# First tokens of each batch written by one DMA each from two queues, between the whole rows, and a third pair of half rows inside layer two

## The chip, the core and the metric

The kernel runs on one core of a Trainium2 chip. The core has a matrix engine (PE), a vector engine (DVE), a scalar engine (ACT), GpSimd (POOL) and a sync engine (SP) that here does nothing but issue DMAs; 16 DMA engines move the data. The metric is the device time of one execution in microseconds (us); a kernel's number is the median of its runs. The profile covers one further execution, whose own time stands beside its span.

## What is computed

Causal attention with a cumulative bias over 8 batches, 8 heads, 576 positions and 64 channels, followed by a soft mixture of 8 experts with 4 slots each:

```python
scores = scale * q @ k^T                          # B=8, H=8, S=576, D=64
bias = -(cum[:, None] - cum[None, :])             # cum = cumsum(max(s, 0))
attn = softmax(where(causal, -1e9, scores + minimum(bias, 0)))
x = (attn @ v) reshaped to (4608, 512)            # 4608 = B*S, 512 = H*D
logits = x @ phi                                  # 4608 x 32 slots
slot_input = softmax(logits, axis=0).T @ x        # 32 x 512
slot_out[e] = relu(slot_input[e] @ w1[e]) @ w2[e] # 512 -> 1024 -> 512, 8 experts
return softmax(logits, axis=1) @ slot_out         # 4608 x 512, float32
```

The output is 4608 x 512 x 4 bytes = 9.44 MB. Everything after `slot_out` is a product with 32 rows for each token, and the writing of the result.

## The kernel before

The attention and the sums of the mixture take the first 390 us or so, in an order that a planner and a hand-written list set. The change does not touch them. What follows them is written out by hand at the end of the function, in program order on each engine.

**Layer one and layer two of the experts.** `mlp1` and `mlp2` are generators that emit a few matmuls for each step. Layer two is computed in two halves of the 512 output columns; `mlp2(half, eg)` takes eight steps of four products (L986) for one group of four experts and ends with a copy (L989, DVE for `eg` 0 and ACT for `eg` 1). The profile counts two matmul records for each fp32 product, so one step is eight records of L986. `pick(half)` (L995, L996) gathers the finished half into the rows `so`. Once `pick(0)` is done, the left 256 columns of any token can be computed, while layer two still works on the right ones.

**The output.** Three functions write it. A batch has 576 tokens: the first 64, and four chunks of 128.

- `two(b, half)`: for batches b and b+1, the four chunks and one half of the columns. Eight products (L1021), four copies from PSUM by ACT and DVE in turn (`evict`, L1007), four DMAs of 256 KB with 1 KB rows (L1027). Batches 0 to 5 are written that way, the left half during layer two and the right half at the end.
- `whole(b)`: for one batch, the four chunks and all 512 columns. Four products (L1034), four copies, two DMAs of 512 KB with 2 KB rows (L1039). Batches 6 and 7.
- `heads(k)`: for four batches, the first 64 tokens. Four products (L1045) put two batches side by side on partitions 0 to 63 and 64 to 127 of a bank; two copies; and DMAs (L1050), the place of the change.

All DMAs of this part are issued from SP, in program order. `stage` hands out the SBUF buffers that the copies write to and the DMAs read from; their names in the profile (`pre`, `arena`, `wg`, `ww`) are those of the weights that lay there. A DMA is issued when the copies that fill its buffer are done and when the DMA that was issued eight places before it has landed (the DMA semaphores are handed round in eight). `banks` takes PSUM banks from a pool of six, and after `late_banks` is set every second call takes two of them from the tiles `y` and `sum`.

The products with `et` and `dn` need nothing of layer two but `so`.

Of the kernel before, what the change touches and what calls it, by code (L numbers as in the profile page):

```python
# [112 lines left out]
def tile_attn_softmoe(ctx: ExitStack, tc, qk, v, s, phi, w1, w2, cst, out):  # L113
    nc = tc.nc
# [3 lines left out]
    B = NT // S  # L118
# [820 lines left out]
    def mlp1(eg):  # L939
        pss = [bank(f"m1{eg}{half}") for half in range(F // 512)]  # L940
        for cc in range(NCC):
            for half in range(F // 512):
                for g in range(4):
                    nc.tensor.matmul(pss[half][32 * g:32 * g + 32, :], st["in"][:, cc, :],  # L944
                                     w1q[4 * eg + g, cc][:, 512 * half:512 * half + 512],
                                     start=(cc == 0), stop=(cc == NCC - 1))
            yield
        relu(eg, pss)
# [31 lines left out]
    def mlp2(half, eg):  # L980

        ps = psy.tile([128, 512], F32, tag=("y", "sum")[eg], name=f"m2{half}{eg}")[:, 0:HC]
        for fc in range(NFC):
            for g in range(4):
                w = w2q[4 * eg + g, 2 * half + fc // 4]
                nc.tensor.matmul(ps[32 * g:32 * g + 32, :], ht[eg][:, fc, 32 * g:32 * g + 32],  # L986
                                 w[:, HC * (fc % 4):HC * (fc % 4) + HC], start=(fc == 0), stop=(fc == NFC - 1))
            yield
        (nc.scalar.copy if eg else nc.vector.tensor_copy)(sos[half][:, eg, :], ps)  # L989

    def pick(half):

        ps = bank(f"sel{half}")
        for eg in range(2):
            nc.tensor.matmul(ps[:, 0:HC], sel[eg], sos[half][:, eg, :], start=(eg == 0), stop=(eg == 1))  # L995
        nc.scalar.copy(so[:, HC * half:HC * half + HC], ps[:, 0:HC])  # L996

    def steps(it, n=100):
        for _ in range(n):
            next(it, None)  # L1000

    outb = out.rearrange("(b t) c -> b t c", b=B)
    turns = [0, 0]

    def evict(dst, src):
        turns[0] += 1
        (nc.scalar.copy if turns[0] % 2 else nc.vector.tensor_copy)(dst, src)  # L1007

    def banks(n):
        turns[1] += 1  # L1010
        if turns[1] % 2 == 0 and late_banks:
            return [bank("po") for _ in range(n - 2)] + [psy.tile([128, 512], F32, tag=t, name="po") for t in ("y", "sum")]
        return [bank("po") for _ in range(n)]

    def two(b, half):

        c = slice(HC * half, HC * half + HC)
        po = [x.rearrange("p (b c) -> p b c", b=2) for x in banks(4)]
        for i in range(2):
            for x, r in zip(po, rows):  # L1020
                nc.tensor.matmul(x[:, i, :], et[r, b + i, 0:128], so[r, c], start=True, stop=True)  # L1021
        for j in (0, 2):
            ot = stage.pop(0).rearrange("p (b j c) -> p b j c", b=2, j=2)
            for x in range(2):
                evict(ot[:, :, x, :], po[j + x])
            for i in range(2):
                nc.sync.dma_start(out=outb[b + i, 64 + 128 * j:320 + 128 * j, c].rearrange("(j p) c -> p j c", p=128),  # L1027
                                  in_=ot[:, i])

    def whole(b):  # L1030

        po = banks(4)
        for x, r in zip(po, rows):
            nc.tensor.matmul(x, et[r, b, 0:128], so[r, :], start=True, stop=True)  # L1034
        for j in (0, 2):
            ot = stage.pop(0).rearrange("p (j c) -> p j c", j=2)
            for x in range(2):
                evict(ot[:, x, :], po[j + x])
            nc.sync.dma_start(out=outb[b, 64 + 128 * j:320 + 128 * j].rearrange("(j p) c -> p j c", p=128), in_=ot)  # L1039

    def heads(k):

        po = banks(2)
        for i, r in enumerate(rows):
            nc.tensor.matmul(po[i // 2][64 * (i % 2):64 * (i % 2) + 64, :], dn[r, k, 0:64], so[r, :], start=True, stop=True)  # L1045
        ot = stage.pop(0).rearrange("p (j c) -> p j c", j=2)
        for x in range(2):
            evict(ot[:, x, :], po[x])
        for i in range(2):
            nc.sync.dma_start(out=outb[4 * k + 2 * i:4 * k + 2 * i + 2, 0:64, :],  # L1050
                              in_=ot[:, i, :])

    late_banks = False
    so = again[left[0]][:, 0:DM]
# [2 lines left out]
    m = mlp1(0)  # L1057
# [6 lines left out]
    m = mlp1(1)  # L1064
# [10 lines left out]
    m = chain(mlp2(0, 0), mlp2(0, 1))  # L1075
# [3 lines left out]
    m = chain(mlp2(1, 0), mlp2(1, 1))  # L1079
# [2 lines left out]
    steps(m, 1)  # L1082
    NA = 6
    for b in range(0, NA, 2):
        if b == NA - 2:
            steps(m)
        two(b, 0)
        steps(m, 5)
    pick(1)
    late_banks = True  # L1090
    for b in range(NA, B):
        whole(b)
    for k in range(2):
        heads(k)
    for b in range(0, NA, 2):
        two(b, 1)
# [51 lines left out]
```

## Time and profile before

| | us |
|---|---|
| runs: lowest, median, highest | 449.62, 449.91, 452.2 |
| the profiled execution: its own time | 450.64 |
| its span, first to last instruction | 448.9 |
| outside the span (450.64 - 448.9) | 1.7 |
| PE busy in the span | 404.2 (90%) |
| TensorE clock granted, mean | 0.956 |

The page's second part cuts the span into 40 slices of 11.2 us. PE is busy in nearly every one of them up to the 37th; in the last three it does nothing, and the row of the DMA engines is the only one that is not empty. Shares of the whole span say nothing of these slices: the stage at the end has its own limits, and it is read from windows of one or a few microseconds. A row of such a table has the stretch, its length, the busy time of PE, PE's weight loads, DVE, ACT and POOL with the number of instructions, the granted clock, the mean busy share of the 16 DMA engines, and what they moved in GB/s.

### The profile page before, as it was taken

How to read it: one execution, taken by the hardware profiler on the slowest of the kernel's cores; microseconds unless marked ns; L12 is line 12 of the kernel's file. 1: busy time of each engine (PE TensorE's matmuls, PEld its weight loads, DVE VectorE, ACT ScalarE, POOL GpSimd, SP SyncE). 2: the span in 40 equal slices, each digit the busy share in tenths (PEclk: the TensorE clock that was granted, in tenths of full speed). 3: DMA queues.
4: the chain of work that ended last, by engine and by line, in shares of the span. 5: the costliest groups of instructions: out<-in, count | busy, mean ns of one | idle time of the engine just before them, and what ended most of it. 6: DMA issues, size and time to landing. Idle time of an engine off the chain costs nothing.

```text
span 448.9 us, 14778 instructions
## 1 busy us (share of the span) xinstructions
PE 404.2 (90%) x5705; PEld 300.4 (67%) x5705; DVE 298.7 (67%) x1018; ACT 241.2 (54%) x717; POOL 282.0 (63%) x385
## 2 busy tenths in 40 slices
PE   7899999989899999999999999999999999999000
PEld 7777877776677777776777777777678683555000
DVE  6777767987887788788868787787885551225100
ACT  2136676676657567666676676758557431125100
POOL 7349889878858887888788879877887200000000
PEclk9599999999999999999999999999999999999655
DMA  5217555626754485448455843532277999988245
GB/s 172 89 56 224 164 174 152 202 78 185 213 153 128 139 231 175 132 127 220 148 156 148 234 129 127 159 114 84 80 191 227 287 407 406 408 326 296 93 141 197
DMA packets 52893, 82.72 MB, mean 184 GB/s; under 512 B 5464, under 2 KB 38744, under 8 KB 52824
## 3 DMA queue, kind: packets, MB, share of 16 engines
q1 hardware_dynamic: 52824, 81.79, 57.7%
q8 instruction: 45, 0.74, 0.6%
q14 instruction: 24, 0.20, 0.2%
HBM read 71.38 MB, written 10.03 MB: 181 GB/s over the span
## 4 chain that ended last, share of the span: by engine, by line
PE 75%; DVE 7%; DMA 4%; issue 2%; POOL 2%; SPq 1%; ACT 1%; DVEq 0%
PE s L384 21%; PE y L485 18%; PE mx L318 11%; PE sum L514 3%; PE m L986 3%; PE m L944 3%; DMA arena<-rs 3%; PE busy L900 2%; DVE nmin L707 2%; PE nat L555 2%; PE lt L627 2%; PE sl L745 1%; DVE arena L547 1%; PE mt L353 1%; PE po L1021 1%
## 5 line engine op out<-in xcount | busy, mean ns | idle before, releaser
L330 DVE CUSTOM_DVE_ANT_0 junk<-mx,arena 128x448 bf16<-128x448 f32 (+3 forms) x320 | 125.6, 427 | 55.0 <-POOL arena L402 26.1
L395 ACT ACTIVATE arena<-s 128x288 f32<-128x288 f32 (+4 forms) x384 | 114.3, 406 | 30.8 <-PE s L384 30.0
L384 PE MATMUL s<-w 64*128 64x288 f32 (+4 forms) x1152 | 109.2, 304 | 0.0
L485 PE MATMUL y<-arena 128*64 128x512 f32 (+4 forms) x640 | 90.2, 427 | 0.0
L384 PEld LDWEIGHTS s<-w 64*128 64x128 f32 (+1 forms) x1152 | 81.7, 177 | 10.1 <-issue 1.2
L402 POOL TENSOR_SCALAR_AFFINE_SELECT arena<-arena 128x256 f32<-128x256 f32 (+1 forms) x160 | 66.6, 430 | 21.9 <-ACT arena L395 20.0
L485 PEld LDWEIGHTS y<-arena 128*64 128x64 f32 x640 | 42.9, 137 | 45.9 <-issue 35.1
L428 POOL TENSOR_TENSOR arena<-arena 128x896 f32<-128x896 f32 x31 | 67.8, 2188 | 7.5 <-PE mt L353 5.3
L318 PE MATMUL mx<-w 64*128 64x288 f32 (+4 forms) x384 | 58.6, 312 | 4.4 <-DVE e_nat L672 2.7
L384 PE MATMUL s<-g 64*128 64x288 f32 (+4 forms) x384 | 56.5, 291 | 0.0
L318 PE MATMUL mx<-g,ones 64*128 64x288 f32 (+4 forms) x384 | 54.9, 304 | 1.0 <-POOL g L228 1.0
L430 POOL TENSOR_TENSOR arena<-arena 128x640 f32<-128x640 f32 x31 | 48.0, 1549 | 2.6
L290 DVE TENSOR_TENSOR w<-arena,w 128x576 fp32r<-128x576 f32 x64 | 48.2, 778 | 0.0
L285 ACT CAST w<-arena 128x576 fp32r<-128x576 f32 x64 | 39.8, 676 | 15.4 <-DMA arena<-in_qk_dram 15.4
L318 PEld LDWEIGHTS mx<-w 64*128 64x128 f32 x384 | 40.5, 189 | 8.6 <-PE s L384 3.8
L497 ACT COPY arena<-y 128x512 f32<-128x512 f32 x32 | 18.8, 588 | 46.1 <-PE y L485 46.1
L318 PEld LDWEIGHTS mx<-g,ones 64*128 64x128 f32 x384 | 40.4, 190 | 1.7 <-POOL g L228 1.2
L384 PEld LDWEIGHTS s<-g 64*128 64x128 f32 (+1 forms) x384 | 35.1, 176 | 0.6
L345 POOL TENSOR_SCALAR mh<-mx 128x10 fp32r<-128x10 f32 x32 | 21.2, 661 | 19.3 <-DVE mx L330 19.2
L432 POOL TENSOR_TENSOR arena<-arena 128x384 f32<-128x384 f32 x31 | 31.4, 1014 | 2.4
L547 DVE TENSOR_TENSOR arena<-arena 128x576 f32<-128x576 f32 x30 | 29.2, 984 | 4.5 <-DMA arena<-rs 4.2
L330 DVE CUSTOM_DVE_ANT_0 junk<-mx,arena,mx 128x288 bf16<-128x288 f32 x64 | 30.6, 516 | 2.2 <-PE mx L318 1.2
(166 smaller groups left out, 546.9 us busy)
## 6 DMA issues: line engine op xcount, KB each, us to landing
arena<-in_qk_dram SPq DMA_DIRECT2D x32, 576.0 KB
pre<-in_w_dram SPq DMA_DIRECT2D x36, 512.0 KB
arena<-in_w_dram SPq DMA_DIRECT2D x19, 512.0 KB
arena<-rs SPq DMA_DIRECT2D x60, 144.0 KB
arena<-in_v_dram SPq DMA_DIRECT2D x32, 256.0 KB
ww<-in_w_dram SPq DMA_DIRECT2D x6, 512.0 KB
out_dram<-pre SPq DMA_DIRECT2D x12, 256.0 KB
out_dram<-arena SPq DMA_DIRECT2D x8, 256.0 KB
```

Source lines behind the costliest of these rows:

```text
L285: nc.scalar.copy(w[:, QO + S * i:QO + S * (i + 1)], st["raw", p][:, i, :])
L290: nc.vector.tensor_tensor(w[:, QO + S * (2 + i):QO + S * (3 + i)], st["raw", p][:, i, :], w[:, QO + S * i:QO + S * (i + 1)].bitcast(F32), ...
L318: nc.tensor.matmul(ps[a][:, d:d + hi - lo], l[r], t[r, KO + lo:KO + hi], start=t is w, stop=t is gt)
L330: nc.vector.tensor_tensor_reduce(out=junk[r, 0:w], in0=ps[r, d:d + w], in1=mask[r, o:o + w], scale=1.0, scalar=m[:, a, 4:5] if i == 1 else ...
L384: nc.tensor.matmul(ps[a][0:n, d:d + hi - lo], t[r, ko + 128 * j:ko + 128 * j + n], t[r, qo + lo:qo + hi], start=x == 0, stop=x == 3)
L395: nc.scalar.activation(st["p", p][0:n, a, o + lo:o + hi], ps[0:n, d:d + hi - lo], AF.Exp, bias=0.0, scale=0.125)
L402: nc.gpsimd.affine_select(d, d, pattern=[[0, 2], [1, n]], compare_op=ALU.is_ge, fill=0.0, base=0, channel_multiplier=-1)
L428: eng.tensor_tensor(z[:, :, 128:576], pt[:, :, 128:576], pt[:, :, 576:1024], op=ALU.add)
L430: eng.tensor_tensor(z[:, :, 256:576], z[:, :, 256:576], pt[:, :, 1024:1344], op=ALU.add)
L432: eng.tensor_tensor(z[:, :, 384:576], z[:, :, 384:576], pt[:, :, 1344:1536], op=ALU.add)
L485: nc.tensor.matmul(y[r, lo - 64:512], vt[:, j, r], st["p", p][:, g, OFF[j] + lo - 128 * j:OFF[j] + 576 - 128 * j], start=(j == 0), stop=(j ...
L547: nc.vector.tensor_tensor(u, u, st.pop(("r", p)), op=ALU.mult)
```

## The change

`heads` writes each batch's first 64 tokens with a DMA of its own: [64, 512] from one half of the partitions, 128 KB, where before one DMA of [2, 64, 512] took two batches from all 128 partitions. Those with even `i` (partitions 0 to 63) are issued from SP, those with odd `i` (partitions 64 to 127) from ACT. `whole` and `heads` alternate: batch 6, heads 0 to 3, batch 7, heads 4 to 7. `two(4, 0)`, which stood behind the last step of layer two, stands four steps after `two(2, 0)` (which itself comes one step earlier), with the remaining six steps of layer two behind it.

```diff
-        for i in range(2):
-            nc.sync.dma_start(out=outb[4 * k + 2 * i:4 * k + 2 * i + 2, 0:64, :],
-                              in_=ot[:, i, :])
+        for i in range(4):
+            (nc.scalar if i % 2 else nc.sync).dma_start(out=outb[4 * k + i, 0:64],
+                                                        in_=ot[64 * (i % 2):64 * (i % 2) + 64, i // 2, :])
...
     NA = 6
     for b in range(0, NA, 2):
-        if b == NA - 2:
-            steps(m)
         two(b, 0)
-        steps(m, 5)
+        steps(m, 4)
+    steps(m)
     pick(1)
     late_banks = True
-    for b in range(NA, B):
-        whole(b)
     for k in range(2):
+        whole(NA + k)
         heads(k)
     for b in range(0, NA, 2):
         two(b, 1)
```

On SP, the DMAs of the end of the program (a row is a line of the kernel, the output, the buffer and the shape of the source as the instruction carries it, for L1050 before the destination's too):

```order
 L1027 DMA out_dram<-pre 128x2x256 x12
 L1039 DMA out_dram<-pre 128x2x512 x2
-L1039 DMA out_dram<-arena 128x2x512
+L1050 DMA out_dram<-arena 64x512 x2
 L1039 DMA out_dram<-wg_6680 128x2x512
-L1050 DMA out_dram<-ww_6779 2x64x512 x4
+L1039 DMA out_dram<-ww_6779 128x2x512
+L1050 DMA out_dram<-ww_6779 64x512 x2
 L1027 DMA out_dram<-wg_6877 128x2x256 x2
 L1027 DMA out_dram<-ww_6945 128x2x256 x2
 L1027 DMA out_dram<-arena 128x2x256 x8
```

The four DMAs of 2x64x512 are gone from SP; four of 64x512 stand there in two pairs, each behind the rows of one whole batch.

On ACT, the copies of the same stretch, with its part of the new DMAs:

```order
 L1007 COPY pre<-po 128x512 x2
 L1007 COPY arena<-po 128x512
+L1050 DMA out_dram<-arena 64x512 x2
 L1007 COPY wg_6680<-po 128x512
 L1007 COPY ww_6779<-po 128x512 x2
+L1050 DMA out_dram<-ww_6779 64x512 x2
 L1007 COPY wg_6877<-po 128x2x256
 L1007 COPY ww_6945<-po 128x2x256
 L1007 COPY arena<-po 128x2x256 x4
```

ACT has two pairs of DMAs among its copies, where it had none; three copies stand behind the first pair before the second comes, and six behind the second.

On PE, layer two's products for the right columns (`m_7372`, `m_7450`) and the products of the output among them (`po`):

```order
-L986 MATMUL m_7372<-pre,wg_6570 32x256 x14
+L986 MATMUL m_7372<-pre,wg_6570 32x256 x10
 L1021 MATMUL po<-pre,e_nat 128x256 x8
-L986 MATMUL m_7372<-pre,wg_6570 32x256 x4
-L986 MATMUL m_7450<-pre,ww_6573 32x256 x16
+L986 MATMUL m_7372<-pre,wg_6570 32x256 x8
+L986 MATMUL m_7450<-pre,ww_6573 32x256 x8
+L1021 MATMUL po<-pre,e_nat 128x256 x8
+L986 MATMUL m_7450<-pre,ww_6573 32x256 x8
 L986 MATMUL m_7450<-pre,ww_6573 32x256
 L986 MATMUL m_7450<-pre,ww_6573 32x256 x3
```

The third group of eight output products moved from behind the last step of layer two to six steps before it.

## Rows read from the trace of the kernel before

**Rows 1.** The page's second part, the span in 40 slices: busy tenths of PE and of the DMA engines, and GB/s.

```profile
span 448.9 us, 14778 instructions
PE   7899999989899999999999999999999999999000
DMA  5217555626754485448455843532277999988245
GB/s 172 89 56 224 164 174 152 202 78 185 213 153 128 139 231 175 132 127 220 148 156 148 234 129 127 159 114 84 80 191 227 287 407 406 408 326 296 93 141 197
```

**Rows 2.** The end of the span in windows (columns as told above: stretch, length, PE, weight loads, DVE, ACT, POOL, clock, DMA share, GB/s).

```profile
399.00:406.00 7.00, 7.00 (x128) 4.08 (x124) 2.05 (x4) 1.61 (x4) 0.00 (x0) 1.00 0.86 294
406.00:407.00 1.00, 1.00 (x14) 0.63 (x7) 0.39 (x1) 0.44 (x1) 0.00 (x0) 1.00 0.35 125
407.00:408.00 1.00, 0.61 (x3) 0.19 (x1) 0.90 (x2) 0.99 (x3) 0.00 (x0) 1.00 0.01 5
408.00:408.20 0.20, 0.13 (x4) 0.13 (x8) 0.00 (x0) 0.02 (x1) 0.00 (x0) 1.00 0.00 0
408.20:411.00 2.80, 2.51 (x22) 1.11 (x26) 1.73 (x3) 1.77 (x4) 0.00 (x0) 1.00 0.97 330
411.00:416.00 5.00, 5.00 (x62) 3.37 (x54) 4.44 (x8) 3.73 (x8) 0.00 (x0) 1.00 1.02 375
417.00:418.00 1.00, 0.00 (x0) 0.00 (x0) 0.36 (x1) 0.00 (x0) 0.00 (x0) 1.00 0.18 37
418.00:431.00 13.00, 0.00 (x0) 0.00 (x0) 0.00 (x0) 0.00 (x0) 0.00 (x0) 0.56 0.14 48
431.00:436.00 5.00, 0.00 (x0) 0.00 (x0) 0.00 (x0) 0.00 (x0) 0.00 (x0) 0.50 0.68 232
441.00:444.00 3.00, 0.00 (x0) 0.00 (x0) 0.00 (x0) 0.00 (x0) 0.00 (x0) 0.50 1.02 346
445.00:447.00 2.00, 0.00 (x0) 0.00 (x0) 0.00 (x0) 0.00 (x0) 0.00 (x0) 0.50 0.14 48
447.60:448.00 0.40, 0.00 (x0) 0.00 (x0) 0.00 (x0) 0.00 (x0) 0.00 (x0) 0.50 0.01 3
448.00:448.90 0.90, 0.00 (x0) 0.00 (x0) 0.00 (x0) 0.00 (x0) 0.00 (x0) 0.50 0.00 0
```

**Rows 3.** SP's DMA issues in order of time, from 409 us to the end, merged by line (start, time from the first issue to the end of the last, number of issues).

```profile
410.03 0.97 SPq L1039 DMA_DIRECT2D out_dram<-pre  x2
411.22 0.99 SPq L1039 DMA_DIRECT2D out_dram<-arena  x1
412.31 1.48 SPq L1039 DMA_DIRECT2D out_dram<-wg  x1
413.89 12.43 SPq L1050 DMA_DIRECT2D out_dram<-ww  x4
...
434.44 8.57 SPq L1027 DMA_DIRECT2D out_dram<-arena  x8
```

**Rows 4.** What one issue takes on SP, by line (shortest, median and longest in ns; first and last start).

```profile
L1050 SPq DMA_DIRECT2D out_dram<-ww x4: 1005/2980/5168, 413.9 to 421.6; - x4
L1039 SPq DMA_DIRECT2D out_dram<-pre x2: 372/372/373, 410.0 to 410.6; - x2
```

**Rows 5.** The first DMA of the third pair of left halves as SP issued it.

```profile
407.36 0.37 SPq L1027 DMA_DIRECT2D out_dram<-pre  x1
```

**Rows 6.** The chain of waits in order of time (start, length, what).

```profile
398.08 2.30 PE m L986 x40
400.37 1.07 PE po L1021 x16
401.45 4.02 PE m L986 x72
405.47 1.11 PE po L1021 x16
406.58 1.05 ACT pre L1007 x2
...
407.64 0.38 ACT pre L996
...
408.07 1.18 PE po L1034 x8
...
416.08 0.68 DVE arena L1007
416.77 0.60 DVEq L1144
```

**Rows 7.** The gathering of the right half on PE, and ACT's copies from layer two's end to the first copy of the last group (start, length, number, and in brackets the idle time before).

```profile
406.48 1.13 PE L995 MATMUL sel<-pre 128*128 128x256 f32 x4
...
405.54 0.37 ACT L989 COPY pre<-m 128x256 f32<-128x256 f32 x1 [3.00 <-PE m L986]
...
413.64 0.59 ACT L1007 COPY wg<-po 128x512 f32<-128x512 f32 x1 [0.72 <-PE po L1021]
```

**Rows 8.** The start of the program: the first DMA, a load to 64 partitions (64 x 576 x 4 bytes), the one behind it, and the windows in which its data moved.

```profile
0.79 0.60 SPq L184 DMA_DIRECT2D arena<-in_s_dram  x1
1.44 0.56 SPq L454 DMA_DIRECT2D arena<-in_v_dram  x1
...
2.00:2.20 0.20, 0.20 (x2) 0.20 (x2) 0.10 (x1) 0.07 (x1) 0.20 (x3) 1.00 0.22 35
2.20:2.60 0.40, 0.40 (x4) 0.40 (x3) 0.00 (x0) 0.00 (x0) 0.34 (x4) 1.00 0.72 109
2.60:3.00 0.40, 0.40 (x4) 0.40 (x3) 0.00 (x0) 0.00 (x0) 0.40 (x1) 1.00 0.87 315
2.00:3.00 1.00, 1.00 (x6) 1.00 (x6) 0.10 (x1) 0.07 (x1) 0.94 (x5) 1.00 0.68 177
```

## The prediction

> **What bounds the kernel now.** I began with the 40 slices [rows 1]. PE is busy to the 37th and then stops; the last three are the DMA engines' alone, and not at their pace: 93 to 197 GB/s against 406 to 408 a little earlier. The chain of waits ends with a DVE copy at 416.8 us [rows 6]: after it no engine computes, and 32 us of the span are output on its way. So the question is what the DMA engines do from 399 us on, and windows answer it [rows 2]. From 411 to 416 us all 16 are busy (share 1.02) at 375 GB/s. At 417 the rate falls to 37, and from 418 to 431 us it is 48 GB/s at a share of 0.14, which is 0.14 x 16 = 2.2 engines. SP's issues say whose DMAs these are [rows 3]: the four of `heads` (L1050, source 2x64x512), issued from 413.89 us on, and they keep SP for 12.43 us, up to 5.17 us for one [rows 4], where others take 0.37. The last column halves, all evicted by 416.8 us, are only issued behind them, the last eight from 434.4 us on.
>
> It looks as if these DMAs lay on two engines, at some 24 GB/s each. That can be tested on the end. Two engines have to move all heads, 8 x 64 x 2048 B = 1.05 MB, at 48 GB/s: 21.8 us; and a sixteenth each of what else comes from 411 us on, 2.10 MB of whole rows and 3.15 MB of half rows: 0.131 MB at 375/16 = 23.4 GB/s and 0.197 MB at 346/16 = 21.6, together 5.6 + 9.1 = 14.7 us. 411.0 + 21.8 + 14.7 = 447.5. The last data moves just before 447.6, and after 445 the rate is again 48 at a share of 0.14 [rows 2]: two engines finish alone. This is the bound of the whole end, from 411 us on.
>
> [...]
>
> **Heads, 128 KB each.** What a DMA from 64 partitions does is not in this stretch. The nearest row is the first load of the program, 64 x 576, issued at 0.79 us with the next behind it at 1.44 [rows 8]: from 2.2 to 2.6 us the share is 0.72, or 11.5 engines, with at most those two in flight. So it is spread over far more than two, and I take all 16. Then nothing holds the two engines back, and from 411 us on the sum is one of bytes: (2.10 + 1.05) MB in 2 KB rows at 375 GB/s is 8.4 us, 3.15 MB in 1 KB rows at 346 is 9.1 us [rows 2], 17.5 in all. That the engines stay fed is shown by 408.2 to 416 us: SP issues faster (0.37 us) than 256 KB move (0.7 us).
>
> Bounds of the rates: all at 375 gives 16.8 us, 0.7 less; all at 294, the mean from 399 to 406 us with its waits for copies in it, gives 21.4, 3.9 more. For the heads alone, the window from 2 to 3 us with 177 GB/s is the lowest that a load to 64 partitions bears: 5.9 us in place of 2.8, 3.1 more. I take 375, since it is of stores with the same 2 KB rows.
>
> [...]
>
> **The start of the run of bytes.** The first whole rows are issued at 410.03 us [rows 3]. A DMA issued at 407.36 [rows 5] moved nothing by 408.2 [rows 2], then all engines: 0.8 us. So on an idle queue the first whole row moves at 410.9, where now it queues behind the third pair until 411.0. I take 411.0.
>
> **The third pair, six steps earlier.** Layer two's 5 + 9 steps take 2.30 and 4.02 us, 0.45 each, and a `two` 1.1 [rows 6]. `two(2, 0)` comes one step earlier, at 399.9, and `two(4, 0)` at 399.9 + 1.1 + 4 x 0.45 = 402.8 in place of 405.5. Its four DMAs follow those of `two(2, 0)` and fill the DMA hole from 406.4 to 408.2 us (5 GB/s at 407) [rows 2]; they are through at 409, and a hole of 2 us opens behind them, until the whole rows come. PE's work before `pick(1)` is the same, 406.6 us at its end. What changes is the cover: now `two(4, 0)` hides ACT's copy of layer two's last sums (0.37 us), while its own copies hold ACT 1.05 us and `pick`'s copy waits for them (406.58 to 407.64) [rows 6, 7]. Afterwards the second half of the gathering waits for that copy, and nothing stands ahead of `pick`'s. Between -0.2 and +0.5 us; I take 0. So this part is worth nothing: it empties the queue earlier, and what follows is not ready earlier.
>
> **ACT's DMAs.** No DMA was issued from ACT before. Its cost there is between SP's 0.37 and 1.48 us for a 512 KB issue into a full queue [rows 3, 4]: 1.5 to 5.9 us for four. Behind the first pair stand three copies, behind the second the six of the last half rows, and PE waits for these to free banks. The cover: whole rows and heads move until 411.0 + 8.4 = 419.4, so the first half row must be copied by about 418.2; its first copy ended at 413.64 + 0.59 = 414.2 [rows 7]. That is 4.0 us: 0 at the low end, 1.9 us at the high. I take 0, nearer to the 0.37, as ACT's own queue is empty. SP no longer waits there.
>
> **Sum.** 411.0 + 17.5 = 428.5 us, and from the last data to the end 448.9 - 447.6 = 1.3 [rows 2]: a span of 429.8, 19.1 less. On the profiled execution's 450.64 that is 431.5; the median of the runs is 0.7 lower, so **430.8 us**.
>
> **Rivals.**
> - *The split does not spread the heads.* If 64x512 lay on two engines as well, the sum is that of now, 411.0 + 36.5 + 1.3 = 448.8 span, 449.8 us. For it: nothing of this shape is a store in the trace. Against: 11.5 engines for a load.
> - *All heads on one engine.* The slower end: the two queues would not matter, engine 0 has 1.05 MB at 24 GB/s, 43.7 us, and its 14.7: 411.0 + 58.4 + 1.3 = 470.7 span, 471.7 us. It decides as soon as a head uses fewer than two engines. Against it the same row.
> - *Heads one at a time.* If each needs its 0.8 us from issue to first data and 0.35 us to move with nothing else beside it, eight take 9.2 us in place of 2.8: 437.2 us. [...] Against it: the 256 KB DMAs, eight in flight, leave no gap from 411 to 416 us.
> - *ACT held.* If ACT waits at its second pair beyond the cover, the DMA engines run dry before the half rows: 1.9 us by the bound above, with the low rates some 4 to 5: 433 to 436.
>
> **Chances.** Forecast 0.87 (429 to 434.7, by the bounds of the rates), ACT held 0.05, one at a time 0.04, no spread 0.03, one engine 0.01. The range goes from 428.8 (all at 375 and the copies 0.5 earlier, with 0.8 for the runs' scatter) to 436. About 1% is what a measurement here can tell from no change. The first three end under 445.4, faster by over 1%: 0.96; no spread is within 1%, 0.03; one engine is slower, 0.01.
>
> **What would show it.** In the profile after: no window of 48 GB/s; share about 1 from 411 to 428 us with the rate near 375, then near 346; SP's four L1050 under 1.5 us each; a hole between 409 and 411; DMA and engines ending together within a microsecond or two, and a span near 430. Wrong would be a stretch at a share near 0.14 or below (rivals one and two), holes among the L1050 (three), or ACT idle before its third-last group of copies with an empty DMA row about 418 us (four).

## The result and the profile after

| | before | after |
|---|---|---|
| median of the runs, us | 449.83 (449.62 to 452.2) | 433.65 (432.28 to 434.59) |
| ratio, with its 95% interval | | 0.9626 [0.9585, 0.9668] |
| the profiled execution | 450.64 | 433.64 |
| its span | 448.9 | 431.9 |

The forecast was 430.8 us with a range to 436: the direction and the mechanism are right, the time is 2.9 us above it. The windows of the end answer to [rows 2] (stretch, length, busy time of PE, weight loads, DVE, ACT and POOL, clock, DMA share, GB/s):

```profile
399.00:406.00 7.00, 7.00 (x123) 3.98 (x119) 3.46 (x6) 2.45 (x5) 0.00 (x0) 1.00 0.89 304
409.00:410.00 1.00, 1.00 (x12) 0.21 (x8) 0.33 (x1) 0.38 (x1) 0.00 (x0) 1.00 0.47 165
410.00:411.00 1.00, 1.00 (x11) 0.45 (x6) 1.00 (x3) 1.00 (x3) 0.00 (x0) 1.00 0.00 0
411.20:414.00 2.80, 2.58 (x20) 0.61 (x13) 2.34 (x4) 1.05 (x4) 0.00 (x0) 1.00 0.98 353
414.00:417.00 3.00, 2.00 (x28) 1.52 (x28) 2.07 (x4) 0.56 (x2) 0.00 (x0) 1.00 0.93 282
417.00:419.00 2.00, 0.99 (x12) 0.79 (x14) 0.41 (x1) 1.63 (x4) 0.00 (x0) 1.00 1.03 380
419.00:421.00 2.00, 0.63 (x8) 0.20 (x4) 1.29 (x2) 1.40 (x3) 0.00 (x0) 0.66 0.90 280
421.00:430.00 9.00, 0.00 (x0) 0.00 (x0) 0.00 (x0) 0.00 (x0) 0.00 (x0) 0.50 1.00 342
430.00:430.60 0.60, 0.00 (x0) 0.00 (x0) 0.00 (x0) 0.00 (x0) 0.00 (x0) 0.50 0.39 135
430.60:431.90 1.30, 0.00 (x0) 0.00 (x0) 0.00 (x0) 0.00 (x0) 0.00 (x0) 0.50 0.00 0
```

The 13 us at 48 GB/s and a share of 0.14 are gone. A hole opens between 409.5 and 411.2 us, as forecast; then all engines work to the end. But twice, from 414 to 417 and from 419 to 421 us, the rate is 280 GB/s at a share of 0.9: the engines are busy and move less. By the order of issue these are the two stretches of the heads. From 421 us on the rate of the half rows is 342 GB/s, where it was 346 before [rows 2].

SP's and ACT's issues of the heads answer to [rows 4] (shortest, median, longest in ns; first and last start in us), and ACT's waits show what the second queue did (time in total, times, longest):

```profile
L1050 ACTq DMA_DIRECT2D out_dram<-arena x2: 547/752/958, 411.3 to 411.9; - x2
L1050 SPq DMA_DIRECT2D out_dram<-arena x2: 768/1168/1569, 411.5 to 412.3; - x2
L1050 ACTq DMA_DIRECT2D out_dram<-ww x2: 474/474/474, 414.6 to 416.8; - x2
L1050 SPq DMA_DIRECT2D out_dram<-ww x2: 1004/1204/1404, 416.5 to 417.6; - x2
```

```profile
ACT wg L1007 <- DMA out_dram<-arena: 2.8, 1, 2.8
ACT wg L1007 <- DVE wg L1007: 1.7, 1, 1.7
```

No issue takes more than 1.6 us, where SP stood up to 5.2 at one before. ACT's copies stood twice. At the first pair it was 1.7 us, of which its two issues themselves are 1.5 (547 and 958 ns; the view names the copy of DVE that came last). At the second pair it was 2.8 us: the two issues take 0.47 us each, but the second begins 2.2 us after the first (414.6 and 416.8), when a DMA issued earlier from `arena` has landed. ACT's next copy and the next products wait behind that.

### The profile page after: what moved, and what is told of

It is laid out like the page before. It is cut to its first block, busy times and chain, and to the rows that moved or that the text cites. A ratio compares the mean times of both kernels' runs of the same rounds, so it can differ in the third digit from the quotient of the medians.

```text
span 431.9 us, 14782 instructions
## 1 busy us (share of the span) xinstructions
PE 405.5 (94%) x5705; PEld 299.6 (69%) x5705; DVE 299.2 (69%) x1018; ACT 240.8 (56%) x717; POOL 281.4 (65%) x385
## 4 chain that ended last, share of the span: by engine, by line
PE 77%; DVE 7%; DMA 6%; issue 3%; POOL 2%; SPq 2%; ACT 1%; DVEq 0%; ACTq 0%
PE s L384 22%; PE y L485 17%; PE mx L318 12%; DMA arena<-rs 4%; PE m L986 3%; PE m L944 3%; PE sum L514 3%; PE busy L900 2%; DVE nmin L707 2%; PE nat L555 2%; PE lt L627 2%; PE sl L745 2%; SPq L524 1%; PE mt L353 1%; DVE arena L547 1%
## 5 line engine op out<-in xcount | busy, mean ns | idle before, releaser
L345 POOL TENSOR_SCALAR mh<-mx 128x10 fp32r<-128x10 f32 x32 | 20.2, 630 | 19.5 <-DVE mx L330 19.5
```

## Experiments

The executions differ in when they reach the middle of layer two: `pick`'s first gathering (L995) begins at 391.6 to 397.8 us among the profiles of this study, with code ahead of it that is the same in all. Beside the ratio, the table has the time from that gathering to the end of the span, for example 431.9 - 395.43 = 36.5 for the changed kernel. It leaves that scatter out, and the readings go by it. Each end is of one profiled execution; how far such ends agree is seen from after, all_sp, pair_late and pool_q, which come to 36.5 or 36.6.

| run | median, us | ratio to before [95%] | first gathering at | from there to the end |
|---|---|---|---|---|
| before | 449.83 | | 395.30 | 53.6 |
| after | 433.65 | 0.9626 [0.9585, 0.9668] | 395.43 | 36.5 |
| split_only | 435.78 | 0.9667 [0.9618, 0.9716] | 397.83 | 37.3 |
| order_only | 449.88 | 0.9990 [0.9963, 1.0017] | 393.28 | 53.3 |
| all_sp | 433.45 | 0.9625 [0.9581, 0.9669] | 394.40 | 36.6 |
| pair_late | 431.60 | 0.9588 [0.9533, 0.9643] | 396.66 | 36.5 |
| wide64 | 432.74 | 0.9609 [0.9566, 0.9651] | 394.78 | 36.3 |
| middle | 434.26 | 0.9643 [0.9594, 0.9691] | 395.15 | 38.4 |
| mid_wide | 433.18 | 0.9607 [0.9559, 0.9656] | 395.22 | 35.9 |
| pool_q | 431.60 | 0.9586 [0.9555, 0.9617] | 393.98 | 36.5 |
| na8 | 433.03 | 0.9626 [0.9583, 0.9669] | 391.58 | 35.6 |
| na8_wide | 433.01 | 0.9608 [0.9564, 0.9652] | 393.88 | 36.0 |
| na8_act_end | 433.04 | 0.9593 [0.9545, 0.9642] | 395.08 | 36.8 |
| na8_mid | 430.14 | 0.9560 [0.9519, 0.9601] | 394.25 | 34.9 |

### What carries the gain: split_only and order_only

```diff
-        for i in range(2):
-            nc.sync.dma_start(out=outb[4 * k + 2 * i:4 * k + 2 * i + 2, 0:64, :],
-                              in_=ot[:, i, :])
+        for i in range(4):
+            nc.sync.dma_start(out=outb[4 * k + i, 0:64],
+                              in_=ot[64 * (i % 2):64 * (i % 2) + 64, i // 2, :])
```

That is all of split_only against the kernel before.

> The kernel before with the four heads DMAs of 64x512 alone, all from SP, behind both whole batches as before, third pair as before. Theory (two engines were the bound, the split alone removes it): 432 to 436 us, no window at 48 GB/s. Rival (the mixing with whole rows or the second queue carries part of the 16 us): 438 us or more.

order_only is the changed kernel with the old two DMAs in `heads`.

```diff
-        for i in range(4):
-            (nc.scalar if i % 2 else nc.sync).dma_start(out=outb[4 * k + i, 0:64],
-                                                        in_=ot[64 * (i % 2):64 * (i % 2) + 64, i // 2, :])
+        for i in range(2):
+            nc.sync.dma_start(out=outb[4 * k + 2 * i:4 * k + 2 * i + 2, 0:64, :],
+                              in_=ot[:, i, :])
```

> The changed kernel with the old heads DMAs (2x64x512, two per group, from SP): only the mixing and the third pair are new. Theory: the two engines have the same work from about 411 us on, 448.5 to 451 us, and the end at 48 GB/s again. Rival (mixing or the earlier pair is worth something of itself): 447 or less.

The split alone takes the end from 53.6 to 37.3 us; the new order with the old DMAs leaves it at 53.3. So the split is 16.3 of the 17.1 us, and the order is worth the other 0.8 once the split is there. That 0.8 is shown in the profiles alone, where all_sp (all from SP, in the new order) has 36.6 too; in total time the intervals of split_only and the changed kernel overlap. The medians of split_only and order_only lie where the theory put them. Windows of order_only:

```profile
409.00:412.00 3.00, 3.00 (x36) 1.40 (x34) 2.38 (x4) 1.75 (x4) 0.00 (x0) 1.00 0.94 344
412.00:417.00 5.00, 2.60 (x36) 1.96 (x29) 3.68 (x6) 3.13 (x6) 0.00 (x0) 0.89 0.15 39
417.00:420.00 3.00, 0.00 (x0) 0.00 (x0) 0.00 (x0) 0.00 (x0) 0.00 (x0) 0.50 0.94 336
420.50:429.00 8.50, 0.00 (x0) 0.00 (x0) 0.00 (x0) 0.00 (x0) 0.00 (x0) 0.50 0.13 52
```

The stretches at a share of 0.13 to 0.15 now begin behind each whole batch, and the end is as late as before: the two engines have the same sum, wherever their DMAs stand. The windows of split_only show what is left:

```profile
413.30:419.00 5.70, 5.38 (x64) 3.55 (x58) 5.13 (x9) 4.43 (x10) 0.00 (x0) 1.00 1.02 375
420.00:424.00 4.00, 0.00 (x0) 0.00 (x0) 0.00 (x0) 0.00 (x0) 0.00 (x0) 0.54 0.89 218
426.00:433.00 7.00, 0.00 (x0) 0.00 (x0) 0.00 (x0) 0.00 (x0) 0.00 (x0) 0.50 1.01 343
```

Whole rows move at 375 GB/s, half rows at 343, and the heads between them at 218 with the engines busy 0.89 of the time. 1.05 MB at 218 are 4.8 us in place of the forecast's 2.8.

### Whether the wait on ACT costs anything: all_sp and pool_q

```diff
-            (nc.scalar if i % 2 else nc.sync).dma_start(out=outb[4 * k + i, 0:64],
+            nc.sync.dma_start(out=outb[4 * k + i, 0:64],
```

> The changed kernel with all heads DMAs issued from SP. If ACT, held at its DMAs, cost the 2 to 3 us above the forecast: 431 to 432.3 us, and no idle 2.8 us on ACT. If the cause is that a DMA from 64 partitions moves slower (213 to 240 GB/s between 414 and 415 us in the changed kernel): 433.3 to 435 us, since SP issues the same DMAs and one queue has them in order.

pool_q has `nc.gpsimd` for `nc.scalar` in that line.

> The changed kernel with the odd heads DMAs issued from GpSimd, which has nothing to do at the end, in place of ACT. If ACT's waits at its DMAs cost time: 1 to 2 us less than the changed kernel, 431.5 to 432.7 us, from the first whole row to the last data 17.5 to 18.3 us in place of 19.2. If they cost nothing, or if that queue is slower to start: 433 to 435.5 us.

Both take the waits for DMAs from ACT, and neither is faster from the gathering on: 36.6 and 36.5 against 36.5. The expectation of 1 to 2 us from ACT fell, though pool_q's median of 431.60 us lies in its window: that interval overlaps the changed kernel's, and from the first data of the whole rows to the last data pool_q takes 429.0 - 409.9 = 19.1 us, not 17.5 to 18.3. The heads are as slow without it: two windows of all_sp and pool_q over that stretch read

```profile
413.00:416.00 3.00, 2.72 (x36) 2.08 (x30) 2.75 (x5) 2.71 (x6) 0.00 (x0) 1.00 0.94 257
```

```profile
412.00:416.00 4.00, 3.31 (x48) 2.64 (x40) 3.65 (x7) 3.44 (x7) 1.03 (x2) 1.00 0.96 286
```

257 and 286 GB/s at a share of 0.94 and 0.96, with the 282 at 0.93 of the changed kernel between them: busy engines, whichever queue feeds them.

### The third pair: pair_late

```diff
     for b in range(0, NA, 2):
+        if b == NA - 2:
+            steps(m)
         two(b, 0)
-        steps(m, 4)
-    steps(m)
+        steps(m, 5)
     pick(1)
```

> The changed kernel with the third pair of left halves behind the whole of layer two, as before. Forecast (worth nothing, -0.2 to +0.5 us): 433.0 to 434.2 us, with the DMA hole at 406 to 408 us again and none at 409.5 to 411. Rival (it fills 1.8 us of empty DMA time): 435 us or more.

36.5 us from the gathering on, as with the earlier pair: worth nothing, as forecast. Its median is 1.4 us below the expected window and its interval overlaps that of the changed kernel; the profile gives no reason for a gain.

### Why the heads move slowly: wide64, middle, mid_wide

wide64 is the kernel before with this in `heads`:

```diff
+        for i in range(2):
+            nc.sync.dma_start(out=outb[4 * k + i:4 * k + i + 3:2, 0:64].rearrange("b t c -> t b c"),
+                              in_=ot[64 * i:64 * i + 64])
```

> The kernel before with two heads DMAs of [64,2,512] per group (256 KB, one from partitions 0 to 63, one from 64 to 127), behind both whole batches, all from SP: the split alone with half as many DMAs of twice the size. The split alone moved its heads at 205 to 217 GB/s. If that rate is a matter of the small size: 300 GB/s or more here and some 2 us less. If it is a matter of 64 partitions on one side: 205 to 220 again and the same time, 433 to 437 us.

The first window is the stretch of its first heads DMA (partitions 0 to 63), the second comes behind it:

```profile
416.50:417.50 1.00, 0.00 (x0) 0.00 (x0) 0.34 (x1) 0.00 (x0) 0.00 (x0) 1.00 1.00 229
417.70:418.90 1.20, 0.00 (x0) 0.00 (x0) 0.00 (x0) 0.00 (x0) 0.00 (x0) 1.00 0.99 345
```

Twice the size hardly lifts the rate of the first: 229 GB/s at a share of 1.00, against 218 with 128 KB in split_only. So the size alone is not the cause. Yet the end is 1.0 us shorter than with 128 KB DMAs at the same place (36.3 against 37.3), and behind the first DMA lies a stretch at 345. By the order of issue and the bytes (256 KB at 229 GB/s are 1.1 us) that stretch is the DMA from 64 to 127 and the start of the next one from 0 to 63. Why it was not slow is open; the expectation of 205 to 220 throughout did not hold.

The run also tells something of the two engines of the old DMAs. 256 KB with the shape 64x2x512 keep all engines busy (a share of 1.00), where 256 KB with the shape 2x64x512 had a share of 0.14, or 2.2 engines [rows 2]; the 64x512 of split_only has 0.89. So the share went with the shape; by what rule, no run shows.

middle puts one batch of each bank on partitions 32 to 95 and the other on 0 to 31 and 96 to 127, from two products of 32 rows each:

```diff
+            for h in range(2):
+                o = 96 * h if i % 2 else 32 + 32 * h
+                nc.tensor.matmul(po[i // 2][o:o + 32, :], dn[r, k, 32 * h:32 * h + 32], so[r, :], start=True, stop=True)
...
+        for j in range(2):
+            nc.sync.dma_start(out=outb[4 * k + 2 * j, 0:64], in_=ot[32:96, j, :])
+        for h in range(2):
+            for j in range(2):
+                nc.sync.dma_start(out=outb[4 * k + 2 * j + 1, 32 * h:32 * h + 32], in_=ot[96 * h:96 * h + 32, j, :])
```

> The split alone with another place of the heads in SBUF: the even batch of a bank on partitions 32 to 95 (one DMA of 128 KB), the odd one on 0 to 31 and 96 to 127 (two of 64 KB). If the slow rate comes from taking one half of the partitions, the DMAs from 32 to 95 run at 330 to 375 GB/s with 84 ns a packet. If it comes from 64 partitions as such, whichever: some 210 GB/s for them too.

As a version it loses: twelve DMAs of 128 and 64 KB leave the engines without work, 141 to 199 GB/s at a share of 0.50 to 0.60 from 418 to 423 us, and the end is 1.1 us longer than with the split alone. But two windows, in the turns of the DMAs from 32 to 95 of the first and the second group, answer the question:

```profile
416.80:417.30 0.50, 0.00 (x0) 0.00 (x0) 0.40 (x1) 0.00 (x0) 0.00 (x0) 1.00 0.96 361
419.70:420.00 0.30, 0.00 (x0) 0.00 (x0) 0.00 (x0) 0.00 (x0) 0.00 (x0) 0.50 0.92 355
```

DMAs of the same 128 KB and the same shape that run at 218 GB/s from the halves in split_only run at 355 to 361 from the middle. mid_wide has the same places with DMAs of two batches:

```diff
+        nc.sync.dma_start(out=outb[4 * k:4 * k + 3:2, 0:64].rearrange("b t c -> t b c"), in_=ot[32:96])
+        for h in range(2):
+            nc.sync.dma_start(out=outb[4 * k + 1:4 * k + 4:2, 32 * h:32 * h + 32].rearrange("b t c -> t b c"),
+                              in_=ot[96 * h:96 * h + 32])
```

> As the run with the heads on partitions 32 to 95, 0 to 31 and 96 to 127, but with two batches in one DMA: 256 KB from 32 to 95, 128 KB each from 0 to 31 and 96 to 127, behind both whole batches, from SP. With the same 256 KB from 0 to 63 the rate fell to some 220 to 236 GB/s at a share of 0.95. If one half of the partitions is the cause: 330 GB/s or more at a share near 1 while the DMA from 32 to 95 moves, and a fall while the others do. If 64 partitions are too few wherever they lie: some 230 at a share near 1 for it as well.

Its windows, in turn of the first group's DMA from 32 to 95, its two others, the second group's from 32 to 95 (the rate rises where its turn is), and its two others:

```profile
416.80:417.40 0.60, 0.00 (x0) 0.00 (x0) 0.47 (x1) 0.00 (x0) 0.00 (x0) 1.00 1.06 393
417.30:418.20 0.90, 0.00 (x0) 0.00 (x0) 0.00 (x0) 0.00 (x0) 0.00 (x0) 1.00 0.94 282
418.70:419.30 0.60, 0.00 (x0) 0.00 (x0) 0.00 (x0) 0.00 (x0) 0.00 (x0) 1.00 1.02 382
419.40:420.00 0.60, 0.00 (x0) 0.00 (x0) 0.00 (x0) 0.00 (x0) 0.00 (x0) 0.97 0.89 219
```

The same 256 KB from 64 partitions run at 393 and 382 GB/s when they are the middle ones, and at 229 when they are the first half. So it is not the number of partitions, nor the size alone: it is which partitions they are. This is shown for 0 to 63, and for the two halves in turn in split_only; for 64 to 127 by itself it is not. Which DMA was on the way in a window is read from the order of issue and the bytes; the trace doesn't name a packet's DMA. Why the halves are slower no run shows. What the windows give is 218 to 229 GB/s against 355 to 393, some 0.6 of it; the stretch at 345 in wide64 does not fit.

### Versions that might beat the changed kernel: na8, na8_wide, na8_act_end, na8_mid

All eight batches are written in two halves, which gives the DMA engines another 1.05 MB to move before the gathering, where the changed kernel has its hole:

```diff
-    NA = 6
+    NA = 8
     for b in range(0, NA, 2):
         two(b, 0)
-        steps(m, 4)
+        steps(m, 3)
     steps(m)
     pick(1)
     late_banks = True
-    for k in range(2):
-        whole(NA + k)
-        heads(k)
     for b in range(0, NA, 2):
         two(b, 1)
+        if b < 4:
+            heads(b // 2)
```

In na8 the heads are those of all_sp.

> All eight batches in two halves (no whole rows), the fourth pair's left halves too inside layer two, heads from SP behind the first and the second pair of right halves. The DMA engines then have 1.05 MB more to move before the gathering and the hole of 1.5 to 2 us closes; the 1.05 MB move in 1 KB rows at 346 in place of 2 KB rows at 375 GB/s, 0.25 us more. 430.5 to 432.5 us. If the hole is without cost because something else sets the end: 433 to 434.

na8_wide has wide64's.

> All batches in two halves, and two heads DMAs of [64,2,512] per group from SP between the right halves. The all-halves version with 128 KB heads took 21.8 us from pick's copy on ACT to the end of the span, the changed kernel 23.9. If fewer and longer heads DMAs help beside 1 KB rows as they did behind the whole rows (1.0 us): 20.8 to 21.5 us there. If the interleaving had that already: 21.6 to 22.

na8_act_end issues the DMAs from partitions 64 to 127 from ACT when all copies are done:

```diff
+        nc.sync.dma_start(out=outb[4 * k:4 * k + 3:2, 0:64].rearrange("b t c -> t b c"), in_=ot[0:64])
+        odd.append((k, ot))
...
+    for k, ot in odd:
+        nc.scalar.dma_start(out=outb[4 * k + 1:4 * k + 4:2, 0:64].rearrange("b t c -> t b c"), in_=ot[64:128])
```

> The same with the DMAs from partitions 64 to 127 issued from ACT behind all its copies, so that they run beside DMAs of 128 partitions on another queue and nothing waits behind them. If two queues mix the packets of one half with others: 20.5 to 21.3 us from pick's copy to the end. If the half DMAs cost the same beside others: 21.6 to 22.2.

na8_mid has mid_wide's heads.

> All batches in two halves (what closes the hole before the gathering) together with the heads on partitions 32 to 95, 0 to 31 and 96 to 127 in DMAs of two batches, from SP between the right halves. The first took 21.8 to 22.2 us from pick's copy on ACT to the end of the span, the second 23.5, the changed kernel 23.9. If the two gains add up: 21.2 to 21.8 us there, and a median of 430 to 432.5 us, since pick's copy itself lies between 405.4 and 410.2 us in the executions profiled so far. If one makes the other idle: 21.8 to 22.4.

The expectations count from `pick`'s second copy. That flatters these versions by the fourth pair's 1.1 us on PE, which now lies before that copy; the table's column counts from the first gathering and does not. By it na8 gains 0.9 us, na8_wide 0.5, na8_act_end loses 0.3, and na8_mid gains 1.6, each in one execution. By the expectations' own measure na8_wide took 22.2 us and na8_act_end 23.0, both above either of their windows, and na8_mid 21.0, below the window for the two gains added up. na8's median, 433.03 us, lies in the window of its rival, that the hole is without cost; neither it nor those of na8_wide and na8_act_end is told apart from the changed kernel's. The hole nearly closes in na8, which has one thin window of 190 GB/s where the changed kernel has 165 and 0:

```profile
400.00:409.00 9.00, 8.54 (x116) 4.41 (x108) 4.23 (x8) 3.90 (x8) 0.00 (x0) 1.00 1.01 342
409.00:410.00 1.00, 1.00 (x12) 0.21 (x8) 0.87 (x2) 0.91 (x2) 0.00 (x0) 1.00 0.56 190
```

na8_mid is the best median of the study, 430.14 us, 0.9560 [0.9519, 0.9601] against 0.9626 [0.9585, 0.9668]. The intervals overlap, so in total time it is not told apart from the changed kernel; in the profile its end is 34.9 us against 36.5.

## Why the prediction was right, and by what it missed

**What bounds the kernel now** held. order_only has the change without the split, and the two engines set its end as before: ratio 0.9990, [0.9963, 1.0017].

**The spread of 64x512** held. The nearest row, a load to 64 partitions at a share of 0.72 [rows 8], was the right one: the share of the heads is 0.89 in split_only. The first two rivals, no spread and one engine, fell with it.

**The bytes** were mis-sized. The forecast had 17.5 us from the first whole row to the last data; it was 430.5 - 411.2 = 19.3. The half rows are as forecast (342 GB/s against 346). The term that failed is the heads at 375 GB/s: I took the rate of the 2 KB rows, which left from 128 partitions, for DMAs that leave from one half of them. Alone they run at 218, and among whole rows the two stretches at 282 and 280 GB/s cost (375 - 282) x 3 / 375 + (375 - 280) x 2 / 375 = 1.3 of the 1.8 us; the last 0.6 us at 135 GB/s and a share of 0.39, where not all engines have work to the end, are most of the rest. The other end of the bound, 177 GB/s and 3.1 us [rows 8], held the case: the split alone gives 4.8 - 2.8 = 2.0. That was luck: the 177 is a mean over the start of a load, from 35 GB/s to 315, and not what DMAs from one half of the partitions move. No row before had a store from one half.

**The halves** do not move at the full rate of 375 GB/s together or apart: 218 alone in split_only, 282 beside whole rows in the changed kernel. The split wins since 218 is over four times 48. The rival of heads one at a time (9.2 us) fell as well: alone they took 4.8.

**The start** was 411.2 for 411.0, and the cover of the gathering cost what the bounds allowed: `pick`'s second copy begins at 408.04 against 407.64, of which 0.13 was there at the first gathering; 0.3 us in the range of -0.2 to +0.5. That the third pair is worth nothing held in pair_late, and the hole came where it was put.

**ACT held** came to pass as a wait (2.8 and 1.7 us) and cost nothing, which is the cover that the prediction named: all_sp and pool_q, without the waits, end as late.

**The end** was the 1.3 us of before. The sum: 0.2 for the start, 1.8 for the bytes and 0.1 from rounding make the span's 431.9 - 429.8 = 2.1 us. The other 0.8 of the median's 2.9 is that I moved the forecast down by the 0.7 us by which the profiled execution of before lay above its median; this kernel's profiled execution lies at its median.

## What to carry to other kernels

When a rate falls, multiply the mean share of the DMA engines by 16: the share of 0.14 was 2.2 engines here. The slow transfer on few engines went with its shape: 256 KB as 2x64x512 had a share of 0.14, and as 64x2x512 one of 1.00. The slow one with the engines busy went with which partitions its bytes left, 229 GB/s from 0 to 63 and 382 to 393 from 32 to 95. In before, split_only and wide64, half rows of 1 KB moved at 343 to 349 GB/s and whole rows of 2 KB at 375 to 376. For a store like this one, try the shape with the long dimension outermost, and look at which partitions it leaves: the middle 64 moved at 355 to 393 GB/s, about as fast as the 375 from 128, the first half, and the two halves in turn, at 218 to 229, some 0.6 of that. When no row shares the property in doubt, here a store from one half of the partitions, the forecast should say so, and its range should hold a rate well below that of the nearest row.

## What was not expected of the hardware

Two things. The rate of the heads went with which 64 partitions their DMAs read: 218 to 229 GB/s from the halves in turn and from the first, 355 to 393 from 32 to 95. And the scatter of the runs (432.3 to 434.6 us here, 428.6 to 433.8 for na8_mid) seems to be made before the change's place: the first gathering begins at 391.6 us in the execution whose DMAs moved 393 GB/s from 350 to 390 us, and at 397.8 in the one with 359, with the others nearly in order between. Two windows of that stretch, of na8 and of split_only, show it:

```profile
350.00:390.00 40.00, 40.00 (x559) 22.99 (x559) 16.11 (x39) 8.74 (x25) 0.46 (x1) 1.00 1.02 393
```

```profile
350.00:390.00 40.00, 38.77 (x525) 22.25 (x525) 15.29 (x38) 11.96 (x37) 2.24 (x6) 1.00 0.96 359
```

The matrix engine is nearly as busy in both (40.0 and 38.8 us), but what the DMA engines load in that time arrives at another pace. That the pace sets the time of the gathering is not shown, since a program that runs ahead also loads earlier; why the executions differ was not tried.
